# Pooled keys, query loads and value loads moved in an attention and two-layer expert kernel: a change of order

## The chip, the cores and the metric

The kernel runs on one core of one Trainium2 chip. The time is device microseconds (us) of one execution. Five engines appear by these names: PE (TensorE matmuls; PEld is its weight load), DVE (VectorE), ACT (ScalarE), POOL (GpSimd) and SP (SyncE, which here only issues DMAs; SPq is its queue).

## The reference, cut to what matters

Three stages follow each other. Keys and values are summed in groups of eight rows (576 rows become 72) before the attention; the attention's output, 4608 rows of 512, goes through a gated product and two more products, and then through a top-1 mixture of eight experts.

```python
    k_p = k.reshape(B, H, Sp, pool, D).mean(axis=3)
    v_p = v.reshape(B, H, Sp, pool, D).mean(axis=3)
    scores = scale * np.matmul(q, k_p.transpose(0, 1, 3, 2))
    ...
    a = x @ w1
    b = x @ w2
    h = a * b @ w3
    return (h @ w_out).astype(np.float32)
    ...
        mask = e_idx == e
        h = np.maximum(x[mask] @ w1[e], 0.0)
        out[mask] = gate_w[mask, None] * (h @ w2[e])
```

Sizes: batch 8, 8 heads, 576 rows, head dimension 64; 512 x 1024 weights in the middle stage; experts of 512 x 1024 x 512.

## The kernel before, in words

The 4608 rows are nine chunks of 512, a chunk is four tiles of 128. A batch is 576 rows, so chunks and batches do not line up: a chunk touches two batches, and a tile can lie half in one batch and half in the next.

Each chunk goes through a **first product** (`mm1`: eight steps m = 0 to 7, each 24 matmuls against w1 and w2, into PSUM tiles `w`) and a **second product** (`mm_w`: four tiles i = 0 to 3, each 48 matmuls against the folded weight W = w3 times w_out, into `x2ps`). Each product is split into three matmuls of high and low parts. The attention of the chunk that follows is spread between these steps by hooks, which are lists of functions called behind a step.

The attention of a chunk is the class `Attention`. `S(i)` does the scores of tile i (eight matmuls `sc<-kblk,q`, L270; sixteen if the tile lies in two batches) and its softmax (DVE L282 to L293, ACT L290, POOL L299). `K(i)` makes sure that the pooled keys of the batches of tile i stand in `kblk`; this is `prep_k` (four DVE sums `ks<-kr`, L183, and two DVE scalings `kblk<-ks`, L188), which also asks for the next batch's raw keys `kr` (four DMAs, L173). `V1` sums the values on POOL, `T` transposes the softmax, `V` multiplies it with the values. `load_q(t)` asks for the queries of tile t (one DMA, L254, two buffers); `early_v(b)` asks for the raw values of a batch (ten DMAs: four `vr<-v_in` of 256 KB at L195 and six small ones at L199).

In a loop chunk (loop variable ch = 1 to 7) the hooks of `mm1` hold `S(0)` to `S(3)` of chunk ch + 1 behind m = 0 to 3, `V1` behind m = 4 and `T` behind m = 5 to 7. The hooks of `mm_w` hold `V` behind i = 0 and 2 and `early_v` behind i = 3. Behind each i a row block is copied by ACT (`x<-x2ps`, L565), four gate columns are added by DVE (`lg<-x2ps,bias`, L566), and the block is stored (`x2d<-x`, L567, on SP).

The order on each engine in these loop chunks is that of the code, and each engine and SP take their instructions in that order. Chunk 0 (ch = 0, `first_chunk`) and all before it are put in order by a scheduler instead. There the weights are converted: 64-bit words `stage` and `cv` are loaded (L428, L387), passed between ACT (L394, L396), DVE (L397, L399), ACT (L400) and POOL (L122), and w3 and w_out are multiplied (`w_fold`, PSUM tiles `wps`). Small set-up work stands in the same place: a memset `zero` and four stores of it (L526, L528), `bias` (L522 to L524), `tri` (L509).

Of the kernel before, what the change touches and what calls it, by code (L numbers as in the profile page):

```python
# [17 lines left out]
B, H, S, D = 8, 8, 576, 64  # L18
# [74 lines left out]
def _program(outer, tc, nc, I, out):  # L93
# [10 lines left out]
    def mm_ps(name, shape=(P, 512)):  # L104
        return psum.tile(list(shape), F32, name=name, tag="mm", bufs=4)
# [4 lines left out]
    def st4(name, shape, dtype):  # L110
        return st.tile(list(shape), dtype, name=name, tag="st4", bufs=7)

    def st2(name, shape=(P, 512), dtype=F32):
        return st.tile(list(shape), dtype, name=name, tag="st2", bufs=2)
# [77 lines left out]
    def load_v(b, j, vr):  # L192

        if j < 4:
            nc.sync.dma_start(flat(vr), I["v"][b, PK * j:PK * j + P, :])  # L195
        else:
            tail = I["v"][b].rearrange("(a k) x -> a k x", k=PK)[2 * j - 8:2 * j - 6, P:]
            for d in range(3):
                nc.sync.dma_start(flat(vr[2 * TK * d:2 * TK * (d + 1)]), tail)  # L199
# [10 lines left out]
    v_raw = {}  # L210

    def early_v(b):

        if b < B:
            pairs = [st4("vr2", (P, 2, D, POOL), F32) for _ in range(3)]
            v_raw[b] = [pairs[j // 2][:, j % 2] for j in range(6)]
            for j in range(6):
                load_v(b, j, v_raw[b][j])
# [32 lines left out]
    def load_q(t):  # L251
        if t < NT and t not in qs:
            qs[t] = st2("q23", (P, 4, P)) if t in (2, 3) else at.tile([P, 4, P], F32, name="q", tag="q", bufs=2)
            nc.sync.dma_start(qs[t], I["q"][t])  # L254

    def softmax_tile(t):
# [9 lines left out]
        if (r0 + P - 1) // S != r0 // S:  # L266
            segs = [(0, 64, r0 // S), (64, P, r0 // S + 1)]
# [65 lines left out]
    def need(f, b):  # L333
        if b < B and (f, b) not in done:
            done.add((f, b))
            f(b)

    class Attention:
# [19 lines left out]
        def S(self, i):  # L358
            self.K(i)
            self.ex.append(softmax_tile(4 * self.ch + i))  # L360
            load_q(4 * self.ch + i + 1)
            if i < 3:
                self.K(i + 1)

        def T(self, js, banks=None):
# [37 lines left out]
    def run(hooks, n):  # L403
        for f in hooks.get(n, ()):
            f()
# [8 lines left out]
    def prep_w12(m):  # L414
        if m < 8 and m not in done_w:
            done_w.add(m)
            conv(I["w1"][m], flat(wt12[m]["w1h"]), flat(wt12[m]["w1l"]), staged.get((m, "w1")))
            conv(I["w2"][m], flat(wt12[m]["w2h"]), flat(wt12[m]["w2l"]), staged.get((m, "w2")))
# [4 lines left out]
    def stage(srcs):  # L423

        for n, tag in enumerate(("Wh", "Wl")):
            t = wp.tile([P, 4, 512], I64, name="stage", tag=tag)
            for i, (k, src) in enumerate(srcs[4 * n:4 * n + 4]):
                nc.sync.dma_start(t[:, i], src)  # L428
                staged[k] = t[:, i]
# [56 lines left out]
    att = Attention(0)  # L486
# [44 lines left out]
    def mm1(ch, x, hooks):  # L531
        xh, xl = x
        abh = abp.tile([P, 8, 512], F32R, name="abh", tag="abh")
        abl = abp.tile([P, 8, 512], F32R, name="abl", tag="abl")
        for m in range(8):
            w = wt12[m]
            ps = []
            for n in ("w1", "w2"):
                p = mm_ps(n)
                for kb in range(4):  # L540
                    mm3(p, w[n + "h"][:, kb], w[n + "l"][:, kb], xh[:, kb], xl[:, kb], kb == 0, kb == 3)
                ps.append(p)
            a = st2("asb")
            nc.scalar.copy(a, ps[0])
            nc.vector.tensor_tensor(a, a, ps[1], op=ALU.mult)  # L545
            nc.scalar.copy(abh[:, m], a)  # L546
            nc.vector.tensor_tensor(abl[:, m], a, abh[:, m].bitcast(F32), op=ALU.subtract)
            run(hooks, m)
        return abh, abl

    def mm_w(ch, ab, lg, hooks, W):
        abh, abl = ab
        Wh, Wl = W[:2]
        for i in range(4):
            t = 4 * ch + i
            cols = slice(P * i, P * i + P)
            pss = [mm_ps("x2ps") for _ in range(2)]
            for m in range(8):
                for l, r in ((abh, Wh), (abh, Wl), (abl, Wh)):
                    for hf in range(2):  # L560
                        nc.tensor.matmul(pss[hf][:, :260], lhsT=l[:, m, cols], rhs=r[:, m, hf], start=m == 0 and r is Wh and l is abh,  # L561
                                         stop=m == 7 and l is abl)
            x2 = st2("x2")
            for hf in range(2):
                nc.scalar.copy(x2[:, 256 * hf:256 * hf + 256], pss[hf][:, :256])  # L565
                nc.vector.tensor_tensor(lg[:, i, 4 * hf:4 * hf + 4], pss[hf][:, 256:260], bias[:, t, 4 * hf:4 * hf + 4], op=ALU.add)  # L566
            nc.sync.dma_start(x2d[P * t:P * t + P, :], x2)  # L567
            run(hooks, i)
# [44 lines left out]
    lgs = [cst.tile([P, 4, E], F32, name=f"lg{i}") for i in range(2)]  # L613
    def first_chunk():
        att = Attention(1)
        h1 = {m: [lambda m=m: prep_w12(m + 2)] for m in range(8)}
        for n, m in enumerate(S1):
            h1[m].append(lambda n=n: att.S(n))
        h1[0] += [lambda: att.K(0)]
        h1[3] += [lambda: stage(fold[:8])]  # L620
        ab = mm1(0, x_first, h1)
        W = w_fold()
        w_gate(*W)
        for n in range(len(S1), 4):
            att.S(n)
        att.V1()
        load_k(2)
        for js in ((0, 1), (2, 3), (4,)):
            sct = psum.tile([P, 2, 512], F32, name="sct", tag="sc", bufs=1)
            att.T(js, {j: sct[:, j % 2] for j in (0, 1, 2, 3, 4, 5)})  # L630
        prep_routing()
        mm_w(0, ab, lgs[0], {0: [att.V], 2: [att.V], 3: [lambda: early_v(2)]}, W)
        return att.x, W

    def next_chunk(ch, x, W):
        att = Attention(ch + 1)
        r = routing(ch - 1, lgs[(ch - 1) % 2])
        sc = []
        h1 = {0: [lambda: sc.append(place(*r)), lambda: att.S(0)], 1: [lambda: att.S(1), lambda: sc[0](0)],
              2: [lambda: att.S(2)], 3: [lambda: att.S(3), lambda: sc[0](1)], 4: [att.V1],  # L640
              5: [lambda: att.T((0, 1)), lambda: sc[0](2)], 6: [lambda: att.T((2, 3))], 7: [lambda: att.T((4,)), lambda: sc[0](3)]}
        ab = mm1(ch, x, h1)
        b = (512 * (ch + 3) - 1) // S
        mm_w(ch, ab, lgs[ch % 2], {0: [att.V], 2: [att.V], 3: [lambda: early_v(b)]}, W)
        return att.x

    x_first = att.x
    x_cur, W = first_chunk()
# [109 lines left out]
    ch = NC_ - 1  # L758
    ab = mm1(ch, x_cur, {})
# [168 lines left out]
```

## Time and profile before

| | us |
|---|---|
| median of three runs | 1324.92 (1324.34 to 1325.64) |
| the profiled execution | 1322.37 |
| its span, first to last instruction | 1320.6 |
| PE busy | 1236.5 (94% of the span) |
| DVE busy | 676.7 (51%) |
| ACT busy | 381.9 (29%) |
| POOL busy | 405.2 (31%) |

A busy PE is not PE at its peak: a matmul's end is modelled, and matmuls overlap. The granted clock of PE is given as a share of its full speed. Loop chunks 1 to 7 run from 205.7 us to 795.3 us of the span.

### The profile page before, as it was taken

The numbers are of one execution on the slowest core, as the hardware profiler recorded it, in microseconds if no ns is written. First come the engines' busy times: TensorE is split into PE (matmuls) and PEld (weight loads), VectorE is DVE, ScalarE is ACT, GpSimd is POOL, SyncE is SP. The second block draws the span as 40 slices with busy tenths as digits, with TensorE's granted clock in tenths as the row PEclk, the third lists the DMA queues.
The fourth block names the chain that finished last, engine by engine and source line by source line (L and its number), as shares of the span: only waits on it lengthen the run. The fifth ranks groups of instructions, "written<-read, shape, count | busy, mean of one in ns | idle before, by whom it ended". The sixth has DMA issues, their size and how long they took to land. (4 is left out here: it accounts for less than half of the span.)

```text
span 1320.6 us, 17555 instructions
## 1 busy us (share of the span) xinstructions
PE 1236.5 (94%) x6518; PEld 1048.9 (79%) x6518; DVE 676.7 (51%) x1325; ACT 381.9 (29%) x813; POOL 405.2 (31%) x463
## 2 busy tenths in 40 slices
PE   4988798999989989999899999999999999999987
PEld 3766577897978979879789798887888888888877
DVE  6999525436344363343543523745464474556442
ACT  5786532322322223223222221211222212222211
POOL 3576301402314014050140301314543344244242
PEclk7989898999999999999999999998999999999998
DMA  8545212012021130210202001305441442344140
GB/s 291 211 167 202 91 49 80 9 65 79 17 77 52 47 97 9 93 44 25 84 1 87 14 25 50 127 24 184 176 170 46 176 176 95 121 175 168 53 170 18
DMA packets 53371, 126.99 MB, mean 96 GB/s; under 512 B 12668, under 2 KB 12924, under 8 KB 53244
## 3 DMA queue, kind: packets, MB, share of 16 engines
q1 hardware_dynamic: 45884, 105.89, 23.2%
q0 software_dynamic: 7232, 19.71, 3.8%
q8 instruction: 57, 0.93, 0.3%
q14 instruction: 54, 0.44, 0.1%
q10 hardware_dynamic: 144, 0.02, 0.0%
HBM read 105.62 MB, written 20.55 MB: 96 GB/s over the span
## 5 line engine op out<-in xcount | busy, mean ns | idle before, releaser
L299 POOL TENSOR_TENSOR ex<-ex,sm 128x576 f32<-128x576 f32 x35 | 40.5, 1157 | 442.8 <-DVE sm L293 423.7
L117 PE MATMUL e<-xh,e1h 128*128 128x512 f32 (+2 forms) x320 | 122.4, 383 | 5.7 <-issue 4.5
L118 PE MATMUL e<-xl,e1h 128*128 128x512 f32 (+2 forms) x320 | 123.0, 384 | 0.0
L117 PE MATMUL w<-xh,w1h 128*128 128x512 f32 x288 | 120.2, 417 | 1.9 <-ACT w1h L400 1.9
L119 PE MATMUL e<-xh,e1l 128*128 128x512 f32 (+2 forms) x320 | 121.4, 379 | 0.6 <-issue 0.6
L119 PE MATMUL e<-e2h,abl 128*128 128x512 f32 x296 | 117.8, 398 | 3.5 <-DVE abl L738 3.5
L117 PE MATMUL e<-e2h,abh 128*128 128x512 f32 x296 | 118.3, 400 | 1.3 <-DVE abl L738 1.3
L119 PE MATMUL w<-xh,w1l 128*128 128x512 f32 x288 | 115.7, 402 | 2.8 <-POOL w1l L122 2.8
L561 PE MATMUL x2ps<-Wh,abh 128*128 128x260 f32 x576 | 117.4, 285 | 0.3 <-ACT Wh L483 0.3
L561 PE MATMUL x2ps<-Wl,abh 128*128 128x260 f32 x576 | 116.6, 283 | 0.0
L118 PE MATMUL e<-e2l,abh 128*128 128x512 f32 x296 | 116.4, 393 | 0.0
L561 PE MATMUL x2ps<-Wh,abl 128*128 128x260 f32 x576 | 115.9, 283 | 0.0
L117 PE MATMUL w<-xh,w2h 128*128 128x512 f32 x288 | 113.3, 393 | 2.8 <-DVE asb L545 2.8
L118 PE MATMUL w<-xl,w1h 128*128 128x512 f32 x288 | 115.4, 401 | 0.0
L545 DVE TENSOR_TENSOR asb<-asb,w 128x512 f32<-128x512 f32 x72 | 49.4, 686 | 126.2 <-PE w L119 79.4
L119 PE MATMUL w<-xh,w2l 128*128 128x512 f32 x288 | 113.3, 393 | 0.0
L118 PE MATMUL w<-xl,w2h 128*128 128x512 f32 x288 | 112.8, 392 | 0.0
L546 ACT CAST abh<-asb 128x512 fp32r<-128x512 f32 x72 | 44.6, 620 | 192.3 <-DVE asb L545 192.3
L737 ACT ACTIVATE abh<-e 128x512 fp32r<-128x512 f32 (+2 forms) x80 | 45.4, 567 | 169.8 <-PE e L119 157.2
L750 POOL DMA_INDIRECT out<-o,idc x37 | 37.5, 1012 | 182.7 <-ACT o L749 161.9
L566 DVE TENSOR_TENSOR lg<-x2ps,bias 128x4 f32<-128x4 f32 x72 | 11.6, 162 | 155.9 <-ACT x L565 151.9
L561 PEld LDWEIGHTS x2ps<-Wh,abh 128*128 128x128 f32 x576 | 89.3, 188 | 0.7 <-ACT Wh L483 0.4
(203 smaller groups left out, 2650.6 us busy)
## 6 DMA issues: line engine op xcount, KB each, us to landing
raw<-ew_in SPq DMA_DIRECT2D x80, 512.0 KB
stage<-w_in SPq DMA_DIRECT2D x19, 512.0 KB
kr<-k_in SPq DMA_DIRECT2D x32, 288.0 KB
q<-q_in SPq DMA_DIRECT2D x36, 256.0 KB
vr<-v_in SPq DMA_DIRECT2D x36, 256.0 KB
x2d<-x SPq DMA_DIRECT2D x36, 256.0 KB
cv<-w_in SPq DMA_DIRECT2D x13, 512.0 KB
vr<-v_in SPq DMA_DIRECT2D x54, 64.0 KB
```

The source lines that it names most:

```text
L117: nc.tensor.matmul(ps, lhsT=wh, rhs=xh, start=start, stop=False)
L118: nc.tensor.matmul(ps, lhsT=wh, rhs=xl, start=False, stop=False)
L119: nc.tensor.matmul(ps, lhsT=wl, rhs=xh, start=False, stop=stop)
L299: eng.tensor_tensor(e3, e3, bc(sm.unsqueeze(2), [P, H, SP_]), op=ALU.mult)
L545: nc.vector.tensor_tensor(a, a, ps[1], op=ALU.mult)
L546: nc.scalar.copy(abh[:, m], a)
L561: nc.tensor.matmul(pss[hf][:, :260], lhsT=l[:, m, cols], rhs=r[:, m, hf], start=m == 0 and r is Wh and l is abh, stop=m == 7 and l is abl)
L566: nc.vector.tensor_tensor(lg[:, i, 4 * hf:4 * hf + 4], pss[hf][:, 256:260], bias[:, t, 4 * hf:4 * hf + 4], op=ALU.add)
L737: nc.scalar.activation(hT[0][:, m, :w], ps[:, :w], AF.Relu)
L750: nc.gpsimd.indirect_dma_start(out=out, out_offset=bass.IndirectOffsetOnAxis(idc[:, i, 0:1], 0), in_=o, in_offset=None, bounds_check=N - 1 ...
```

## The change

Three edits. The sums of the keys of a batch (and with them the request for the next batch's raw keys) go from `S` into the hook behind i = 1 of the second product of the chunk before; in `S` they stay for chunks 0 and 1 alone. `S(i)` asks for the queries of two tiles ahead, not one. `early_v` does nothing for a batch whose values have been asked for (batch 7 came up twice, at ch = 5 and 6).

```diff
     def early_v(b):
-        if b < B:
+        if b < B and b not in v_raw:
...
             self.ex.append(softmax_tile(4 * self.ch + i))
             load_q(4 * self.ch + i + 1)
-            if i < 3:
+            load_q(4 * self.ch + i + 2)
+            if i < 3 and self.ch < 2:
                 self.K(i + 1)
...
         prep_routing()
-        mm_w(0, ab, lgs[0], {0: [att.V], 2: [att.V], 3: [lambda: early_v(2)]}, W)
+        mm_w(0, ab, lgs[0], {0: [att.V], 1: [lambda: need(prep_k, 2)], 2: [att.V], 3: [lambda: early_v(2)]}, W)
...
         b = (512 * (ch + 3) - 1) // S
-        mm_w(ch, ab, lgs[ch % 2], {0: [att.V], 2: [att.V], 3: [lambda: early_v(b)]}, W)
+        mm_w(ch, ab, lgs[ch % 2], {0: [att.V], 1: [lambda: need(prep_k, b)], 2: [att.V], 3: [lambda: early_v(b)]}, W)
```

The order of PE's matmuls is the same in both programs. Lines behind L362 stand one line further down in the changed kernel (L567 is L568 there). On DVE and SP the order moves.

First place, a loop chunk on SP. Before, from the stores of the second product of ch = 3 to the stores of the next one:

```order
L567 DMA x2d<-x_3767 128x512
L567 DMA x2d<-x_3861 128x512
L567 DMA x2d<-x_3917 128x512
L567 DMA x2d<-x_4001 128x512
L195 DMA vr_4007<-v_in 128x512 x2
L195 DMA vr_4008<-v_in 128x512 x2
L199 DMA vr_4009<-v_in 32x1x512 x6
L254 DMA q<-q_in 128x512 x2
L173 DMA kr<-k_in 128x576 x4
L254 DMA q<-q_in 128x512 x2
```

The same stretch of the changed kernel:

```order
L568 DMA x2d<-x_3769 128x512
L568 DMA x2d<-x_3863 128x512
L173 DMA kr<-k_in 128x576 x4
L568 DMA x2d<-x_3934 128x512
L568 DMA x2d<-x_4018 128x512
L195 DMA vr_4024<-v_in 128x512 x2
L195 DMA vr_4025<-v_in 128x512 x2
L199 DMA vr_4026<-v_in 32x1x512 x6
L254 DMA q<-q_in 128x512 x4
```

The key loads moved from among the query loads to between the second and third store; the four query loads are still behind the values, but each is now for a tile one further on.

Second place, the second product of ch = 2 on DVE. Before:

```order
L566 TENSOR_TENSOR lg_400<-x2ps,bias 128x4 x2
L329 TENSOR_TENSOR xl<-avps,xh 128x256 x4
L240 SCALAR_TENSOR_TENSOR vbl<-vs,c,vbh 128x4x64 x2
L247 SCALAR_TENSOR_TENSOR vbt<-vs,c,vbt 32x2x64 x2
L566 TENSOR_TENSOR lg_400<-x2ps,bias 128x4 x4
```

The changed kernel, same place:

```order
L240 SCALAR_TENSOR_TENSOR vbl<-vs,c,vbh 128x4x64 x2
L247 SCALAR_TENSOR_TENSOR vbt<-vs,c,vbt 32x2x64 x2
L567 TENSOR_TENSOR lg_401<-x2ps,bias 128x4 x2
L183 TENSOR_REDUCE ks<-kr 128x72 x4
L188 TENSOR_SCALAR kblk_87<-ks 64x4x72 x2
L567 TENSOR_TENSOR lg_401<-x2ps,bias 128x4 x2
```

The six key instructions stand between the `lg` pair of the second tile and that of the third.

Third place, SP at the end of `w_fold`, in the part that the scheduler puts in order. In brackets are the semaphores that an instruction waits for: DVE, Pool and PE mean an instruction of that engine, DMAHW an earlier DMA. Before:

```order
L528 DMA x2d<-zero 128x512 [waits DMAHW4_49,DVE_49]
L528 DMA x2d<-zero 128x512 [waits DMAHW5_49]
L528 DMA x2d<-zero 128x512 [waits DMAHW6_49]
L528 DMA x2d<-zero 128x512 [waits DMAHW7_49]
L387 DMA cv<-w_in 128x512 [waits DMAHW0_49,PE_49]
L387 DMA cv<-w_in 128x512 [waits DMAHW1_49,PE_49]
L387 DMA cv<-wo_in 128x512 [waits DMAHW2_49,PE_49,Pool_49]
L387 DMA cv<-w_in 128x512 [waits DMAHW3_49,PE_49,Pool_49]
```

The changed kernel:

```order
L529 DMA x2d<-zero 128x512 [waits DMAHW0_49]
L173 DMA kr<-k_in 128x576 [waits DMAHW1_49,DVE_49]
L173 DMA kr<-k_in 128x576 [waits DMAHW2_49,DVE_49]
L388 DMA cv<-w_in 128x512 [waits DMAHW3_49,PE_49]
L388 DMA cv<-w_in 128x512 [waits DMAHW4_49,PE_49]
L388 DMA cv<-wo_in 128x512 [waits DMAHW5_49,PE_49,Pool_49]
L173 DMA kr<-k_in 128x576 [waits DMAHW6_49,DVE_49]
L388 DMA cv<-w_in 128x512 [waits DMAHW7_49,PE_49,Pool_49]
```

The scheduler has drawn `prep_k(2)` forward from the second product of chunk 0 into `w_fold`. Three of the loads for batch 3 now stand ahead of weight loads, and each waits for a DVE sum of batch 2. On DVE the same six key instructions stand there, one sum earlier in `w_fold` and, in the rows below, the rest behind the memset `zero`:

```order
L527 MEMSET zero 128x512
L398 SCALAR_TENSOR_TENSOR stage<-stage 128x512
L183 TENSOR_REDUCE ks<-kr 128x72
L400 SCALAR_TENSOR_TENSOR stage<-stage 128x512
L183 TENSOR_REDUCE ks<-kr 128x72
L398 SCALAR_TENSOR_TENSOR cv<-cv 128x512
L183 TENSOR_REDUCE ks<-kr 128x72
L400 SCALAR_TENSOR_TENSOR cv<-cv 128x512
L188 TENSOR_SCALAR kblk_87<-ks 64x4x72 x2
```

Before, no sum of batch 2 stood in `w_fold`, and the last of the three `bias` instructions (L524, L525 in the changed kernel) came behind the memset; now it comes ahead of it, and the first of them (L522) stands much further up, behind the casts of `mf`.

## Rows read from the trace of the kernel before

**Rows 1.** The page's first part: busy time, share of the span, instructions.

```profile
PE 1236.5 (94%) x6518; PEld 1048.9 (79%) x6518; DVE 676.7 (51%) x1325; ACT 381.9 (29%) x813; POOL 405.2 (31%) x463
```

**Rows 2.** Waits of PE: who waited for whom, total us, times, longest.

```profile
PE sc L270 <- DMA q<-q_in: 18.7, 6, 4.4
PE sc L270 <- DVE kblk L188: 8.9, 5, 5.1
PE sc L270 <- issue: 8.4, 3, 4.3
```

**Rows 3.** Windows, first products of ch = 1 to 7: us, busy (count), PEclk, DMA.

```profile
205.70:262.90 57.20, 52.92 (x252) 44.22 (x250) 29.48 (x67) 14.27 (x26) 18.63 (x33) 0.94 0.14 42
...
456.90:514.90 58.00, 53.50 (x261) 44.34 (x259) 29.68 (x67) 14.38 (x26) 19.96 (x34) 0.97 0.23 68
...
714.90:768.40 53.50, 50.59 (x252) 42.21 (x251) 26.30 (x62) 14.26 (x26) 11.47 (x16) 1.00 0.15 48
sum 397.30, PE 368.82 PEld 306.16 DVE 204.15 ACT 100.19 POOL 128.28; mean PE 52.69 PEld 43.74 DVE 29.16 ACT 14.31 POOL 18.33
```

**Rows 4.** Timeline of PE in ch = 7: start, us, instruction, [idle <-releaser].

```profile
720.42 1.23 PE L270 MATMUL sc<-kblk,q 128*128 128x144 f32 x8
...
730.04 1.22 PE L270 MATMUL sc<-kblk,q 128*128 128x144 f32 x8 [2.91 <-DMA q<-q_in]
...
736.59 1.14 PE L270 MATMUL sc<-kblk,q 128*128 128x144 f32 x8
```

**Rows 5.** Timeline of all engines in ch = 1, around the second score.

```profile
218.80 2.68 DVE L183 TENSOR_REDUCE ks<-kr 128x72 f32<-128x576 f32 x4
...
221.51 0.62 DVE L188 TENSOR_SCALAR kblk<-ks 64x288 f32<-64x288 f32 x2
...
222.24 2.26 PE L270 MATMUL sc<-kblk,q 128*128 128x144 f32 x8 [4.28 <-issue]
```

**Rows 6.** Timeline of PE in ch = 4, the scores.

```profile
462.44 1.23 PE L270 MATMUL sc<-kblk,q 128*128 128x144 f32 x8
...
473.52 2.26 PE L270 MATMUL sc<-kblk,q 128*128 128x144 f32 x8 [4.37 <-DMA q<-q_in]
...
481.49 2.52 PE L270 MATMUL sc<-kblk,q 128*64 128x144 f32 x16
```

**Rows 7.** Timeline of SP in ch = 4, value and query loads.

```profile
461.62 3.95 SPq L199 DMA_DIRECT2D vr<-v_in  x6
465.62 0.89 SPq L254 DMA_DIRECT2D q<-q_in  x2
```

**Rows 8.** Timeline of DVE in the second product of ch = 2.

```profile
366.31 0.44 DVE L566 TENSOR_TENSOR lg<-x2ps,bias 128x4 f32<-128x4 f32 x2 [5.37 <-ACT x L565]
```

**Rows 9.** View of line L183: durations (ns), DVE's idle time before it.

```profile
L183 DVE TENSOR_REDUCE ks<-kr x32: 700/742/753, 3.8 to 659.6; 128x72 f32<-128x576 f32 x32
...
  DMA kr<-k_in: 3.5, 2
```

**Rows 10.** Timeline of DVE at the end of w_fold.

```profile
128.17 0.44 DVE L522 TENSOR_TENSOR bias<-mf,mb 128x288 f32<-128x288 f32 x1
...
129.04 0.48 DVE L526 MEMSET zero<- 128x512 f32 x1
129.45 0.62 DVE L397 SCALAR_TENSOR_TENSOR stage<-stage 128x512 int32<-128x512 int32 x1
130.00 1.56 DVE L524 TENSOR_TENSOR bias<-bias,btmp 128x288 f32<-128x288 f32 x1
```

**Rows 11.** Timeline of SP, the same place.

```profile
129.56 1.80 SPq L528 DMA_DIRECT2D x2d<-zero  x4
131.45 0.90 SPq L387 DMA_DIRECT2D cv<-w_in  x2
```

**Rows 12.** Timelines of ACT and PE, the same place.

```profile
135.81 0.67 ACT L394 ACTIVATE cv<-cv 128x512 f32<-128x512 f32 x1 [1.62 <-DMA cv<-w_in]
...
139.29 0.50 PE L117 MATMUL wps<-wo,w 128*128 128x512 f32 x1 [2.02 <-ACT w L400]
```

## The prediction

> **What bounds the kernel now.** The page's first part comes first: PE is busy 94% of the span, every other engine at most about half of it [rows 1]. So time can only come from PE's idle stretches, or from matmuls that run at the lower clock. The view of PE's waits names the idle stretches [rows 2]: the scores `sc` (L270) waited 18.7 us for queries, six times, and 8.4 us for "issue", three times, where the view found no releaser. The third row, 8.9 us for `kblk`, lies mostly in the start-up; about 1.4 us of it is in the loop. That makes 28.5 us of idle PE in loop chunks 1 to 7.
>
> What stands behind "issue" is read from a timeline [rows 5]: in chunk 1 DVE does four key sums and two scalings (2.68 + 0.62 us), the last ends at 222.13, and PE, idle for 4.28 us, starts the second score at 222.24. So the key sums stand between two scores of the same chunk and PE waits for them. The queries are read in chunk 4 [rows 6, 7]: SP asks for them at 465.62, behind ten value loads, and PE's second score starts at 473.52, 7.9 us after. A step of the first product takes 6.55 us, score to score (736.59 less 730.04, [rows 4]). A load that is asked for behind one score and takes 7.9 us is too late for the next.
>
> Idle time is not all of the loss. After such a wait the same eight score matmuls took 2.26 us, against 1.22 to 1.23 undisturbed [rows 4 to 6], and the mean granted clock was 0.94 and 0.97 in the stretches of chunks 1 and 4, 1.00 in chunk 7 [rows 3]; full is 2.4 GHz, and what it falls to is 1.2. So I price the loss by the length of the seven first products, not by the gaps.
>
> **The change, part by part.**
>
> *The loop's waits.* The seven first products take 397.3 us together [rows 3]. What one takes without a wait comes from chunk 7, 53.5 us, which kept its clock and has one wait: from its first to its second score 9.62 us pass, from the second to the third 6.55, so the wait costs 3.07 and an undisturbed first product is 50.4 us [rows 3, 4]. Chunks 2, 4 and 6 have one tile that lies in two batches, sixteen small matmuls in 2.52 us instead of eight in 1.22 [rows 6]: 1.3 us each of real work. Undisturbed: 7 x 50.4 + 3 x 1.3 = 356.7. The loss is 397.3 - 356.7 = 40.6 us, of which 28.5 is idle PE and 12 is slow clock and restart. In the ratio of the gaps, some 27 of it belongs to the queries and 14 to the keys. If both waits go, all of it goes, since the matmuls themselves stay in the same order.
>
> Do they go? *Keys:* in chunks 2 to 6 every sum now stands in the second product of the chunk before, with two whole tiles of it (2 x 5.8 us, pair to pair of [rows 8]: 5.37 idle and 0.44 work) still to come before any score. *Queries:* the loads stay behind the values on SP, but the first of them is now for the third score, not the second; the second score's tile was asked for behind the fourth score of the chunk before. In chunk 4, the tightest, the load would land at 473.5 as now, and the third score is due at 462.44 + 2 x 6.55 = 475.5: 2 us to spare. The load of two tiles ahead waits on SP for the score that frees its buffer; queued behind it is only the next query load and, much later, the stores. The doubled values (ten DMAs, about 6 us of SP's time in chunk 6) stood ahead of chunk 7's query load; they go, and that gain is within chunk 7's 3.07.
>
> *What covers the moved sums.* In the second product DVE now has 2.68 + 0.62 = 3.30 us more between the second and third `lg` pair. It sat idle for 5.37 us there, waiting for ACT [rows 8], so 2.1 us remain and the third pair is not late. Cover gone, 3.3 us in each of five chunks would be at stake, 16 us, plus the clock. The key loads that follow wait on SP for these sums, with the third store behind them; that store is not due before the third pair.
>
> *The scheduled part, w_fold.* Here the change costs. The six key instructions of batch 2 are drawn forward into a stretch where PE waits for converted weights (2.02 us, [rows 12]), these wait for `cv` data (ACT 1.62 us, [rows 12]), and SP asked for that data at 131.45, straight behind the four zero stores, which waited for DVE's memset [rows 10, 11]. Now three things come ahead. One sum (0.74, the median of [rows 9]) and the last `bias` (1.56) stand ahead of the memset, the first `bias` (0.44) no longer does [rows 10]: 1.9 us later, the memset ends at 131.4. Behind it DVE does twice a conversion (0.62) and a sum (0.74), 2.7 us, to the end of the third sum at 134.1, and only then can SP issue the second key load and, 0.45 later (half of the 0.90 of two loads, [rows 11]), the first `cv` load: 134.6 instead of 131.45, 3.1 us late. I take 3.1 us, since ACT, DVE and PE behind it all wait for that data in turn. Below, if PE's own pace hid the memset's 1.9: 1.4. Above: all 3.30 us of key work, the 1.9, and a longer PE gap that brings the lower clock, another 3: 8.
>
> In chunk 1 the keys' wait goes with that, and its 4.28 us are in the 40.6. In the start-up query loads move ahead of some weight loads; PE waits there on DVE and ACT, which convert, and I count 0, bounds -1 and +1.
>
> *Sum.* 1322.37 - 40.6 + 3.1 = 1284.9 for the profiled execution. The median of the three runs shown, 1324.92, lies 2.55 above the profiled one, which puts the median after at 1287.4; I round to **1288 us**, 2.8% less.
>
> **A rule of the skill against the trace.** The row says that a query load of 256 KB landed 7.9 us after it was asked for, in the shadow of the values [rows 7, 6]. The Trainium skill, "DMA: Bandwidth & Descriptors", section "Anatomy of one DMA", gives a fit (for the GpSimd path) of about 2.0 us plus bytes over 436 GB/s: an estimate of 2.6 us. By that the load of 465.62 would be there at 468.2, before the second score is due, and asking earlier would bring nothing; the trace does not agree, it names the query DMA as PE's releaser in all six cases. If the rule held in place of the row, only the keys' share would go, and that is the fourth rival.
>
> **Rivals.**
>
> 1. *The query wait moves to the third score.* For it: the load is still issued at the same place of SP's queue, with 2 us to spare in chunk 4. Against: one query load, not two, now follows the values at once. If half of the queries' 27 us stayed: 1288 + 14 = 1302.
> 2. *w_fold costs its upper bound.* For it: the key loads stand in the weight loads' way on SP and in the DMA engines, and DVE is full there. 1288 + 5 = 1293, with the longer gap's clock up to 1296.
> 3. *DVE parks on keys in the second product* (the other side). DVE takes its instructions in order; if the sums found the raw keys not landed, every `lg` behind them would be late, the PSUM tiles would not come free, and PE would stop. The place is the third tile of five second products. PE is covered for the 2.1 us of DVE and one tile of 5.8. To lose the 37.5 us that the rest brings, PE must stand 7.5 us per chunk, so the keys must come 15.4 us late. At 18 us late: 1288 + 5 x 10.1 = 1338, slower. Against: all 32 sums of the kernel waited 3.5 us for keys, twice [rows 9], and the keys are now asked for one second product ahead of the next.
> 4. *The query load is not what holds the second score,* the change does not do what it says: 1322.37 - 14 + 3.1 + 2.55 = 1314. Against: the releaser in [rows 2].
>
> **How the numbers follow.** The forecast gets 0.78, with a range of its own from 1283 to 1293 (w_fold from its lower to its upper bound; loss from 39 to 42). Rival 2 beyond that 0.08, rival 1 0.06, rival 4 0.03, rival 3 0.03, no change at all 0.02. The range runs from 1283 to 1297: forecast and rival 2, 0.86. A measurement of this kernel tells 0.2%, about 2.6 us, from no change. Faster by more: 0.95; within: 0.02; slower: 0.03.
>
> **What would show it.** In the profile after: no score in chunks 1 to 7 waits over 0.5 us; the seven first products take about 357 us at clock 1.00; the query row is gone from PE's waits; in w_fold the wait for ACT's `w` grows from 2.0 to about 5 us and SP's first `cv` load of the last group stands near 134.6; DVE's wait for ACT before the third `lg` shrinks to about 2 us. Wrong would be: a wait for `q` before the third score; DVE idle on `kr` in a second product; PE idle on `lg`; or a w_fold longer by over 8 us.

## The result, and the profile after

| | before | after |
|---|---|---|
| median of four executions, us | 1324.63 (1323.27 to 1325.64) | 1280.16 (1276.81 to 1281.75) |
| ratio, 95% interval | | 0.9662 (0.964 to 0.9683) |
| the profiled execution, us (span) | 1322.37 (1320.6) | 1281.75 (1280.0) |
| first products of chunks 1 to 7 together, us | 397.3 | 355.2 |
| `w_fold`, us | 58.1 | 61.2 |

The change wins 44.5 us, 3.4%. The forecast was 1288 us, with a range from 1283 to 1297: the direction is right, the time is 2.8 us below the range.

The page's first part of the kernel after, to be held against [rows 1], shows PE busier by share and with 14 us less of busy time; 13.6 of them lie in the seven first products, where the same matmuls run at a higher mean granted clock:

```profile
PE 1222.4 (96%) x6518; PEld 1040.2 (81%) x6518; DVE 676.3 (53%) x1325; ACT 380.6 (30%) x813; POOL 404.3 (32%) x463
```

PE's waits over the whole span, to be held against [rows 2]. The rows for queries and for "issue" before a score are gone; the row for `kblk` lies in the start-up. Asked for the seven chunks alone (207 to 755 us), the view has no row at all. The wait for converted weights in `w_fold` is the second thing to see (before, 5.2 us in three waits, the longest 2.0):

```profile
PE sc L270 <- DVE kblk L188: 8.1, 4, 5.1
...
PE wps L117 <- ACT w L401: 5.8, 3, 4.5
```

Windows over the seven first products, to be held against [rows 3] (us, busy time and count of each engine, granted clock, DMA share, GB/s). Every window is full of PE, and the granted clock is 1.00, the 2.4 GHz level, in all of them:

```profile
207.30:257.60 50.30, 50.30 (x251) 42.27 (x250) 26.13 (x61) 14.15 (x26) 19.16 (x34) 1.00 0.11 29
...
441.50:492.70 51.20, 51.20 (x260) 42.70 (x259) 26.78 (x61) 14.27 (x26) 20.29 (x34) 1.00 0.18 54
...
677.50:727.90 50.40, 50.40 (x252) 42.36 (x252) 26.32 (x62) 14.15 (x26) 11.58 (x16) 1.00 0.06 17
sum 355.20, PE 355.20 PEld 297.53 DVE 185.85 ACT 99.30 POOL 129.40; mean PE 50.74 PEld 42.50 DVE 26.55 ACT 14.19 POOL 18.49
```

Timelines of PE and of SP in chunk 4, to be held against [rows 6, 7]. SP comes to the queries at 450.32, behind the ten value loads as before, but PE goes from score to score in steps of 6.5 us, and no row has an idle time in brackets:

```profile
446.98 1.23 PE L270 MATMUL sc<-kblk,q 128*128 128x144 f32 x8
453.54 1.14 PE L270 MATMUL sc<-kblk,q 128*128 128x144 f32 x8
460.08 1.74 PE L270 MATMUL sc<-kblk,q 128*64 128x144 f32 x16
...
450.32 18.51 SPq L254 DMA_DIRECT2D q<-q_in  x4
```

Timeline of DVE in the second product of chunk 2, to be held against [rows 8]. The sums stand between the second and the third pair of `lg`, and DVE's wait for ACT ahead of the third pair has shrunk from 5.37 to 2.08 us, as forecast:

```profile
350.51 0.44 DVE L567 TENSOR_TENSOR lg<-x2ps,bias 128x4 f32<-128x4 f32 x2 [3.83 <-ACT x L566]
350.86 2.72 DVE L183 TENSOR_REDUCE ks<-kr 128x72 f32<-128x576 f32 x4
353.62 0.62 DVE L188 TENSOR_SCALAR kblk<-ks 64x288 f32<-64x288 f32 x2
356.31 0.44 DVE L567 TENSOR_TENSOR lg<-x2ps,bias 128x4 f32<-128x4 f32 x2 [2.08 <-ACT x L566]
```

Timelines of SP, ACT and PE at the end of `w_fold`, to be held against [rows 11, 12]. Key loads now stand ahead of and among the last `cv` loads. ACT starts on the `cv` data at 138.76, 2.95 us later than before, and PE's wait behind it is 4.51 instead of 2.02 us:

```profile
131.00 1.33 SPq L173 DMA_DIRECT2D kr<-k_in  x2
132.43 0.88 SPq L388 DMA_DIRECT2D cv<-w_in  x2
...
138.76 0.65 ACT L395 ACTIVATE cv<-cv 128x512 f32<-128x512 f32 x1 [3.78 <-DMA cv<-w_in]
...
142.22 0.79 PE L117 MATMUL wps<-wo,w 128*128 128x512 f32 x1 [4.51 <-ACT w L401]
```

Over the profiled executions, then: loop -42.1 us, `w_fold` +3.1, and a third part that the prediction did not have, `w_gate` behind `w_fold`. These are the windows of `w_gate`, first of the kernel before, then of after; it is 1.4 us shorter, at a higher mean clock:

```profile
154.70:174.90 20.20, 16.42 (x64) 7.00 (x64) 7.96 (x14) 6.69 (x14) 0.00 (x0) 0.83 0.07 26
```

```profile
157.70:176.50 18.80, 14.97 (x65) 6.84 (x65) 7.99 (x14) 6.66 (x14) 0.00 (x0) 0.91 0.09 28
```

No other stage differs by more than 0.9 us, and the sum is -40.6, from 1322.37 to 1281.75.

### The profile page after: what moved, and what is told of

Read it like the earlier page. It is cut to its first block, busy times and chain, and to the rows that moved or that the text cites. A ratio compares the mean times of both kernels' runs of the same rounds, so it can differ in the third digit from the quotient of the medians.

```text
span 1280.0 us, 17551 instructions
## 1 busy us (share of the span) xinstructions
PE 1222.4 (96%) x6518; PEld 1040.2 (81%) x6518; DVE 676.3 (53%) x1325; ACT 380.6 (30%) x813; POOL 404.3 (32%) x463
## 5 line engine op out<-in xcount | busy, mean ns | idle before, releaser
L751 POOL DMA_INDIRECT out<-o,idc x37 | 37.5, 1013 | 184.2 <-ACT o L750 169.9
L705 DVE CAST e1h<-raw 128x512 fp32r<-128x512 f32 x80 | 70.5, 896 | 36.0 <-DMA raw<-ew_in 35.2
```

The lines of the kernel that those rows point to most:

```text
L705: nc.vector.tensor_copy(h2, r)
L751: nc.gpsimd.indirect_dma_start(out=out, out_offset=bass.IndirectOffsetOnAxis(idc[:, i, 0:1], 0), in_=o, in_offset=None, bounds_check=N - 1 ...
```

## The experiments

All ratios are to the kernel before, run in the same set on the same chip. Five sets gave medians of the kernel before from 1314.17 to 1317.58 us, with 62 executions between 1305.61 and 1326.6, so times of different sets are compared by ratio.

**The three parts alone.** Each leaves one part of the diff in the kernel before. Keys alone:

```diff
-            if i < 3:
+            if i < 3 and self.ch < 2:
...
+ 1: [lambda: need(prep_k, 2)]   (second product of chunk 0)
+ 1: [lambda: need(prep_k, b)]   (second product of chunks 1 to 7)
```

(The last two lines show only the entry that is added to the hooks of `mm_w`.)

> The keys' part of the change alone: sums and next loads in the preceding second product; queries loaded one tile ahead, the last batch's values loaded twice, as in the kernel before. Theory (the two kinds of wait in the loop are separate and their prices add): of the 42.1 us that the loop lost, the keys' waits with the half clock behind them are 4.28 + 3.4 in chunk 1, 1.60 in chunk 3, 2.49 + 1.7 in chunk 5, 1.32 in chunk 6, 14.8 together; less 3.1 us in w_fold. About 1312 us (1310 to 1315); the query waits before second scores stay. Rival (a late query alone holds the scores, keys' sums only wait beside it): nothing comes back in chunks 3 to 6, w_fold costs 3.1, 1320 us or more.

Queries alone:

```diff
             load_q(4 * self.ch + i + 1)
+            load_q(4 * self.ch + i + 2)
```

> The query part alone: queries loaded two tiles ahead; keys' sums in the first product and values twice, as in the kernel before. Theory (additive): the query waits with their half clock, about 27.2 us, go; keys' waits stay, w_fold is as before: about 1297.5 us (1295 to 1300). Rival 1 (the sums take over: with the second score on time VectorE's sums for the third are late by what the query wait had hidden): the waits before third and fourth scores grow by 2 to 3 us in each of chunks 3, 5 and 6, 1303 us or more. Rival 2 (query latency is not what holds the second scores): 1315 us or more.

Values alone:

```diff
-        if b < B:
+        if b < B and b not in v_raw:
```

> The guard against the second load of the last batch's values alone. Theory: only chunk 7 is touched, where the query of the second score lies behind ten value loads that are not needed; its wait of 2.91 us goes, with nothing else: about 1321.7 us. Rival (these loads cost nothing or more elsewhere): 1324.6 us, or over 3 us won.

Measured: keys alone 1302.84 us, ratio 0.9894 (0.9853 to 0.9935), 12.5 us won where 12.6 were expected, but by other parts: the seven first products took 386.4 us, 10.9 less where 14.8 were expected, and `w_fold` 59.2, 1.1 more where 3.1 were expected. Queries alone 1300.38, ratio 0.9889 (0.9863 to 0.9915), 15.0 us won where 27 were expected; first products 380.6. Values alone 1306.42, ratio 0.9939 (0.9914 to 0.9964), 8.9 us won where 2.9 were expected. The sums of the seven first products, of keys, queries and values alone:

```profile
sum 386.40, PE 366.15 PEld 305.18 DVE 184.50 ACT 99.96 POOL 130.69; mean PE 52.31 PEld 43.60 DVE 26.36 ACT 14.28 POOL 18.67
```

```profile
sum 380.60, PE 363.42 PEld 303.19 DVE 205.96 ACT 99.71 POOL 129.60; mean PE 51.92 PEld 43.31 DVE 29.42 ACT 14.24 POOL 18.51
```

```profile
sum 390.90, PE 367.48 PEld 305.38 DVE 204.40 ACT 100.09 POOL 129.88; mean PE 52.50 PEld 43.62 DVE 29.20 ACT 14.30 POOL 18.55
```

PE's waits from chunk 1 to 7, of queries alone:

```profile
PE sc L270 <- issue: 10.3, 3, 4.3
PE sc L270 <- DVE kblk L188: 6.8, 3, 3.1
```

and of keys alone:

```profile
PE sc L270 <- DMA q<-q_in: 20.2, 6, 4.9
```

The waits are not separate. With the queries on time, the scores wait for the keys 17.1 us, where the gaps that the keys held were 4.3 + 1.6 + 2.5 + 1.3 = 9.7 us in the kernel before ([rows 5] has the first): the sums now are the later of two things that had been late together; their waits grew by 3.1, 1.9 and 2.3 us in chunks 2, 3 and 4. Queries alone went the way of rival 1, though that had named chunks 3, 5 and 6. The three parts win 10.9, 16.7 and 3.1 us in the first products (the last is chunk 7 alone, 53.5 to 50.4, as expected), 30.7 in sum, against 42.1 together: 11 us come back only when both late things are mended.

What values alone won beyond chunk 7 is not shown to be its doing. Its other first products were 3.3 us shorter in sum (4.1 shorter in chunks 4 to 6, 0.8 longer in 1 to 3), where the edit moves nothing, and the rest lies for the most part in stages behind the loop which differ between executions of one kernel too (below).

**`w_fold`.** Three versions of the changed kernel. Batch 2's sums put back into chunk 1:

```diff
-            if i < 3 and self.ch < 2:
+            if i < 3 and self.ch < 3:
...
- 1: [lambda: need(prep_k, 2)]   (second product of chunk 0)
```

> The changed kernel, with the sums of the third batch (index 2) alone put back where the kernel before had them, in the first product of chunk 1. Theory (w_fold's longer time is the price of these sums and the loads that they call for): w_fold falls from about 61.5 to 57.5 to 58.1 us, the first product of chunk 1 rises from 50.36 to 57.3, the other six stay at 50.36 and 51.25: 3 to 3.5 us more than the changed kernel, ratio to the kernel before about 0.973. Rival (w_fold's length has another cause): w_fold stays at 61 to 62, and the whole is 7 us more, ratio 0.976 or more.

Only the key loads of batch 3 held back, VectorE's order as in the changed kernel:

```diff
-        if 1 < b < B - 1:
+        if 2 < b < B - 1:
             load_k(b + 1)
...
-  4: [att.V1],
+  4: [lambda: load_k(3), att.V1],
```

> The changed kernel, with the four key loads of the next batch (index 3) taken out of the sums of batch 2, and issued in the first product of chunk 1; SyncE's queue in w_fold is then as in the kernel before, VectorE's as in the changed kernel. Theory 1 (the loads ahead of the last conversion loads in SyncE's queue are what lengthens w_fold): w_fold 57.5 to 58.5 us, the rest unchanged, 3 to 4 us less than the changed kernel. Theory 2 (VectorE's sums between the conversions lengthen it): w_fold stays at 61 to 62 us, no difference to the changed kernel beyond 1 us.

The whole second product of chunk 0 in written order:

```diff
-        mm_w(0, ab, lgs[0], {0: [att.V], 1: [lambda: need(prep_k, 2)], 2: [att.V], 3: [lambda: early_v(2)]}, W)
...
     with tc.manual_schedule(engines={ET.PE, ET.DVE, ET.Activation, ET.Pool, ET.SP}):
+        mm_w(0, ab, lgs[0], {0: [att1.V], 1: [lambda: need(prep_k, 2)], 2: [att1.V], 3: [lambda: early_v(2)]}, W); x_cur = att1.x
         for ch in range(1, NC_ - 1):
```

> The changed kernel, with the second product of chunk 0 inside the part whose order is as written, so that neither the sums of batch 2 nor the key loads of batch 3 are drawn into w_fold. Both theories of w_fold's length: w_fold 57.5 to 58.5 us. Theory (sums and loads find room in this second product as they do in the other seven): that stage stays at 30.8 us give or take 0.5, the first product of chunk 1 at 50.4, and the whole is 3 to 4 us less than the changed kernel. Rival (the order as written is worse there, transposes no longer spread by the scheduler, values loaded late): the stage grows by 2 us or more, or the value sums are late in the next first product, and the gain is gone.

Measured: 1279.21 us, ratio 0.9701 (0.9675 to 0.9728); 1270.37, ratio 0.9641 (0.9616 to 0.9667); 1271.87, ratio 0.9649 (0.9626 to 0.9671). Windows of `w_fold` in these three, in this order:

```profile
95.90:153.40 57.50, 48.77 (x193) 36.30 (x194) 45.72 (x54) 39.08 (x68) 33.55 (x23) 0.97 0.46 171
```

```profile
95.70:153.40 57.70, 48.92 (x192) 36.11 (x193) 48.53 (x60) 39.14 (x68) 33.96 (x24) 0.97 0.46 172
```

```profile
96.10:153.30 57.20, 48.64 (x193) 36.30 (x193) 45.48 (x54) 39.05 (x68) 33.72 (x24) 0.97 0.47 173
```

In the second, VectorE still does the sums in `w_fold` (60 instructions, 48.53 us busy, against 54 and 45.72 without them), and the stage is as short as in the kernel before. So the price of `w_fold` is that of SyncE's four key loads, not of VectorE's sums. Timelines of SP and ACT in this second version say how: `cv` loads asked for at 130.18 are used at 134.33, 4.15 us later; in the changed kernel, with key loads around them, it was 132.43 and 138.76, 6.33 us.

```profile
130.18 0.90 SPq L388 DMA_DIRECT2D cv<-w_in  x2
...
134.33 0.67 ACT L395 ACTIVATE cv<-cv 128x512 f32<-128x512 f32 x1 [0.15 <-DMA cv<-w_in]
```

The run with keys alone parts the two costs. There the first `cv` loads are asked for as late, but with one key load behind them and none directly ahead, and their data is used 4.40 us later; `w_fold` is 1.1 us longer. So about 2 us of the price are data that come slower with two key loads directly ahead, and 1 us is the later request:

```profile
132.50 0.90 SPq L387 DMA_DIRECT2D cv<-w_in  x2
133.50 0.40 SPq L387 DMA_DIRECT2D cv<-wo_in  x1
133.99 0.38 SPq L173 DMA_DIRECT2D kr<-k_in  x1
...
136.90 0.66 ACT L394 ACTIVATE cv<-cv 128x512 f32<-128x512 f32 x1 [1.82 <-DMA cv<-w_in]
```

With batch 2 late, chunk 1's first product was 56.5 us (57.3 expected), and the other six undisturbed, as expected; the whole was put at a ratio of about 0.973 and came to 0.9701, no more than the changed kernel's own 0.9701 and 0.9706 in other sets (below). In written order the second product of chunk 0 kept its 30.7 us: the rival there falls.

The kernel before was run once more for a trace, on the same chip.

> The kernel before, unaltered, for its trace on this chip. On the chip of the first four runs its executions had a median of 1315.35 us, where the four shown had 1324.63. Theory (chips and executions differ outside the loop): the seven first products add up to 397 us give or take 2 as in [rows 5], and the difference lies in the stages after the loop, whose waits for transfers are shorter. Rival (the half clock behind the loop's waits comes and goes): the stages after the loop are as in the profiled execution, and the seven first products add up to 392 us or less.

Its profiled execution took 1319.75 us, where its set had a median of 1317.58. Windows of its seven first products, their sum (the row meant in the expectation is the sum in [rows 3]):

```profile
sum 397.10, PE 369.30 PEld 307.02 DVE 206.60 ACT 100.16 POOL 128.96; mean PE 52.76 PEld 43.86 DVE 29.51 ACT 14.31 POOL 18.42
```

The loop is the same to 0.2 us in the two traces; the 2.6 us between them lie elsewhere: chunk 8's first product is 3.4 us shorter (46.1 instead of 49.5), all else together 0.8 us longer.

**The changed kernel again.** Two sets with it unaltered, and one with the held key loads beside it.

> The changed kernel itself, unaltered. Disputed: that its profiled execution (1281.75 us) lay above the other three, where that of the kernel before lay below all its others. Theory (chance of one execution): executions spread over 1277 to 1282 us with the profiled one anywhere among them, the mean granted clock higher where the time is shorter; median 1279 to 1281. Rival (the profile itself costs or gives a fixed amount): the profiled execution stands at the same end again, 1.5 us or more above the median of the others.

> The changed kernel once more, unaltered, beside the next run on the same chip, and for a third sample of the difference to the kernel before, which was 44.5 us in the four executions shown and 38.4 us on the chip of the first four runs. Theory (loop 42.1 us, w_fold 3 to 4 us against it; all else is what executions differ by in the stages before and after the loop): seven first products 355.2 us, difference 36 to 41 us, ratio 0.969 to 0.973. Rival (the change wins several us outside the loop as well): difference 43 us or more, ratio 0.9675 or less.

> The changed kernel with the key loads of batch 3 held back to the first product of chunk 1, unaltered from its first run, beside the changed kernel on the same chip. Theory (these four loads cost 3 to 4 us in w_fold): 3.5 to 6.5 us less than the changed kernel here, w_fold 57 to 58.5 us against 61 to 62. Rival (its 1270.37 us was a good draw of executions): within 2 us of the changed kernel.

Measured: 1276.96 us (1273.63 to 1280.04), ratio 0.9706 (0.9681 to 0.9731), 38.4 us won; 1278.19 (1277.16 to 1280.67), ratio 0.9701 (0.9672 to 0.9731), 39.0 us won; held key loads 1274.28, ratio 0.9671 (0.9641 to 0.9702), 3.9 us less than the changed kernel beside it. The seven first products took 355.2 us in all three traces. What executions of one kernel differ by is shown by two windows, chunk 8's first product and the first quarter of the expert matmuls. The changed kernel, profiled with 1281.75 us:

```profile
754.80:804.00 49.20, 46.50 (x203) 37.90 (x202) 23.82 (x62) 9.72 (x19) 13.52 (x12) 0.97 0.20 70
828.20:946.50 118.30, 113.32 (x499) 91.47 (x498) 65.91 (x160) 23.80 (x41) 47.73 (x42) 0.97 0.38 137
```

and again, with a span of 1274.3 instead of 1280.0 us:

```profile
754.70:801.50 46.80, 45.06 (x205) 36.81 (x203) 24.12 (x62) 9.80 (x19) 13.11 (x12) 1.00 0.21 74
825.60:940.60 115.00, 112.91 (x499) 91.11 (x499) 67.02 (x160) 23.80 (x41) 48.14 (x42) 0.99 0.39 140
```

These two stages make 5.7 us, as much as the whole difference of the spans. The kernel before has the same two kinds of stage, 46.1 or 49.5 us in chunk 8's first product in its two traces. That the change wins several us outside the loop, the rival in the third sample, falls by both ratios.

**Why the query load is late.** Three versions of the kernel before. The ten value loads in another order:

```diff
-            for j in range(6):
+            for j in (4, 5, 0, 1, 2, 3):
                 load_v(b, j, v_raw[b][j])
```

> The kernel before, with the order of a batch's ten value loads turned round: the six loads of 64 KB first, the four of 256 KB behind them; the query load that holds the second score is issued behind all ten, as before. Disputed: why that query takes 7 to 8 us. Theory (the six small loads go over few DMA engines, and the query's packets on these engines stand behind them): with four full-width loads between them and the query, the query lands within about 4 us, the waits before second scores (2.6, 3.4, 4.4, 2.4, 2.9 and 2.9 us in chunks 2 to 7) go to under 1 us; as in the run with queries two tiles ahead, the sums of the keys take part of it over, so about 15 us less than the kernel before, ratio 0.988 to 0.990. Rival (bytes: 1.4 MB stand ahead of the query, whatever their order): the waits stay within 0.5 us of these, ratio 0.998 to 1.002.

The queries on another queue:

```diff
-            nc.sync.dma_start(qs[t], I["q"][t])
+            (nc.scalar if t > 8 else nc.sync).dma_start(qs[t], I["q"][t])
...
-            self.K(i)
+            self.K(i); self.ch > 1 and load_q(4 * self.ch + i + 1)
```

> The kernel before, with the queries from tile 9 on loaded through ScalarE's DMA queue instead of SyncE's, each issued ahead of the exponential of the tile before; ScalarE comes to that place at about the time at which SyncE had issued it (about 297.7 in chunk 2), so only the queue differs, not the time of issue. Disputed: why the query that follows ten value loads needs 7 to 8 us. Theory (it stands behind them in its own queue): on another queue it lands within 3 to 4 us, the waits before second scores fall under 1 us, the keys' waits take over as in the run with queries two tiles ahead, about 15 us less than the kernel before, ratio 0.987 to 0.990. Rival (the DMA engines themselves are full with the values' 1.4 MB, whichever queue asks): waits of 2 to 4.5 us stay in chunks 2 to 7, ratio 0.998 or more.

The small loads with another first dimension (`ext` and the masks in `constants()` are permuted with it):

```diff
-            tail = I["v"][b].rearrange("(a k) x -> a k x", k=PK)[2 * j - 8:2 * j - 6, P:]
+            tail = I["v"][b].rearrange("(a k) x -> a k x", k=PK)[2 * j - 8:2 * j - 6, P:].rearrange("a k x -> k a x")
```

> The kernel before, with the six small value loads of a batch read with the sixteen keys as the first dimension of the source, where it was two heads; masks and the attention's tail columns are permuted to match; the order of all queues and the number of all instructions are as before. Disputed: why a query behind the ten value loads takes 7 to 8 us when their order does not matter and another queue frees it. Theory (these loads go over few of the DMA engines, and the query's packets wait on these): the waits for queries fall from 18.7 us to under 4 in all, the keys' waits take over as on the other queue, ratio 0.987 to 0.993. Rival (the bytes ahead in the queue, however spread): waits of 2 to 4.5 us stay in chunks 2 to 7, ratio 0.998 to 1.002. The Trainium skill, DMA: Bandwidth & Descriptors, section Why a DMA increments its semaphore by 16 and not by 1, is on the theory's side: it has the number of engines as the largest common divisor, up to 16, of both sides' slowest dimensions, 2 for these loads as they were and 16 with the edit.

PE's waits for queries in chunks 1 to 7, another order first, then another queue:

```profile
PE sc L270 <- DMA q<-q_in: 21.3, 6, 4.1
```

```profile
PE sc L270 <- DMA q<-q_in: 1.2, 2, 0.6
```

With another first dimension the view has no such row, only the keys':

```profile
PE sc L270 <- issue: 10.3, 3, 4.3
PE sc L270 <- DVE kblk L188: 6.8, 3, 3.1
```

Measured: order 1320.47 us, ratio 1.0022 (0.9998 to 1.0046); queue 1304.55, ratio 0.9927 (0.9903 to 0.9951); first dimension 1295.5, ratio 0.9857 (0.9828 to 0.9886). What the order was expected to change did not come: with the small loads first, the second score started 7.2 to 8.0 us after its query was asked for, as in the kernel before (7.5 to 8.2), and all ten stand ahead of it in the queue either way. On ScalarE's queue the wait is nearly gone (1.2 of 18.7 us), so they hold it up in their own queue, not by filling the DMA engines for all queues; 9.6 us were won there, where about 15 were expected. And with the same bytes, the same order and the same queue, spread by their first dimension, the small loads hold nothing up: not the bytes, but how the six loads of 64 KB are laid out. In chunk 2 SP asked for the query at 291.64, and the second score started at 296.88 without a wait. The view of the DMAs lists 2.9 us from issue to landing for this load, and a median of 3.0 for the 26 query loads of the window from 203 to 760 us:

```profile
291.64 0.58 SPq L254 DMA_DIRECT2D q<-q_in  x1
...
296.88 1.20 PE L270 MATMUL sc<-kblk,q 128*64 128x144 f32 x8
```

```profile
q<-q_in SPq DMA_DIRECT2D x1, 256.0 KB, 2.9
```

What the small loads do shows in the same view. It has the mean busy share of the 16 DMA engines in tenths, here in 40 slices of 0.225 us around the query of chunk 2. The kernel before, 297 to 306 us (the query asked for at 297.77), with PE's second score and a window of the low stretch (the last two numbers are the DMA share and the GB/s):

```profile
DMA  1111111122799311111111111111111111100875
```

```profile
305.50 3.76 PE L270 MATMUL sc<-kblk,q 128*64 128x144 f32 x16 [2.62 <-DMA q<-q_in]
```

```profile
300.50:304.70 4.20, 2.38 (x11) 1.64 (x9) 3.35 (x7) 1.16 (x2) 0.72 (x1) 1.00 0.13 51
```

The query on ScalarE's queue, the same 297 to 306 us (asked for at 297.20, the score not waiting at 302.87):

```profile
DMA  1111169885111111111111111111111111000558
```

Another first dimension, 291 to 300 us (asked for at 291.64):

```profile
DMA  5714508373597200000000000000000000000876
```

Before, the small loads keep a share of 0.13 of the engines busy, at 51 GB/s; at that rate their 393 KB take 7.7 us, an estimate. A short burst comes between 299.0 and 300.2, but the low level goes on to 304.9, and the score starts 0.6 us later. On the other queue the burst comes too, and the score does not wait for the low level to end; with the other first dimension there is no such level, and all has come by 294.2. So most of the query comes in the burst, and a part of it stands behind the small loads on the few engines that these use. The view gives the mean of all engines and not each one, so this last step is the reading that fits the three traces, not a row.

The Trainium skill, "DMA: Bandwidth & Descriptors", section "Why a DMA increments its semaphore by 16 and not by 1", says that a load runs on as many engines, up to 16, as the largest number that divides the slowest dimension of both its sides: 2 for the small loads as they were, 16 with the edit. The trace agrees: two of 16 engines are a share of 0.125, and the window above has 0.13.

The edit also shortened what lies ahead of `w_fold`, where value loads stand among the weight loads, from 96.6 to 91.7 us, and the seven first products from 397.3 to 383.3, which makes up nearly all of its 19.4 us, more than the other queue won. So it was tried on the best version, the changed kernel with the key loads held back.

> The changed kernel with the key loads of batch 3 held back, and with the small value loads spread as in the run beside it. Theory (in the loop no score waits any more, so nothing is to be had there; only the value loads of batches 0 and 1, which stand among the weight loads ahead of w_fold, could gain): within 1 us of the version with the loads held back alone, ratio 0.963 to 0.968. Rival (the small loads held up weights in the start-up as well): w_fold or the stretch before it 2 us or more shorter, ratio 0.962 or less.

Measured: 1266.04 us (1264.65 to 1270.98), ratio 0.9629 (0.9607 to 0.9651), the fastest of all. Of the rival the stretch ahead of `w_fold` came true: it is 92.3 us (95.7 with the loads held alone). But in these two traces nearly all of it is given back, in `w_fold` (59.2 instead of 57.7) and in `w_gate` (19.4 instead of 17.8), which ends at 170.9 us instead of 171.2. The windows of `w_gate`, first with the loads held alone, then with the small loads spread as well:

```profile
153.40:171.20 17.80, 13.89 (x64) 6.11 (x64) 8.03 (x14) 6.74 (x14) 0.00 (x0) 1.00 0.10 29
```

```profile
151.50:170.90 19.40, 15.50 (x65) 6.21 (x65) 8.00 (x14) 6.66 (x14) 0.00 (x0) 0.91 0.09 27
```

Against the held loads' 0.9641 and 0.9671 the ratio does not settle whether the step pays there.

## Why the prediction was right in direction and wrong in size

*The loop's waits: right.* No score waits in chunks 1 to 7, none moved to the third score (rival 1), the query load was what held the second (rival 4 falls), DVE did not park on keys (rival 3), and DVE's spare 2.1 us ahead of the third `lg` pair came out at 2.08. The loop's share of the `kblk` row was 1.3 us, not 1.4, which changes nothing in the sum. An undisturbed first product was priced at 50.4 us and took 50.4. One size in the term was off: a tile that lies in two batches was priced at 1.3 us, from a 2.52 us row of [rows 6]; it takes 1.74 us where its neighbours take 1.14 to 1.23, and the chunks that hold one are 0.9 us longer than the others. The 2.52 us stood behind a query wait, one tile later, and were set against 1.22 us of an undisturbed tile; in the second trace of the kernel before the same tile took 1.74 us. Three such chunks and rounding make 355.2 instead of 356.7: 1.5 us. That the loss goes as one, not in two shares, the runs of single parts showed; the 27 and 14 us by ratio of the gaps were no prices (16.7 and 10.9 alone).

The fit in the Trainium skill, "DMA: Bandwidth & Descriptors", section "Anatomy of one DMA", an estimate of 2.6 us for that load, is near the 2.9 us that it took once the small loads were spread, though the page has the fit for the GpSimd path and this load is SyncE's; that section says nothing of what stands ahead in the queue, and that was the case here.

*`w_fold`: the sum right, the way there wrong.* The 3.1 us were met in the profiled execution; in two other traces it was 3.6 to 3.8. But the step had the first `cv` load at 134.6, behind a memset that was to end 1.9 us late, and three sums. The memset ended at 129.06, 0.5 us earlier than before; the load was asked for at 132.43, 1.0 us late, and its data came 2 us slower, with key loads ahead of it in the queue. Holding back those loads alone gave all of it back. The data in the key loads' way are the mechanism of rival 2, at the forecast's price: that the two errors cancelled is luck.

*`w_gate`: put at nothing.* The 1.4 us that the profiled pair showed were not in the sum. The stage took 20.2 and 20.3 us in the two traces of the kernel before and 18.8, 19.1 and 19.1 in the three of the changed kernel; but four versions of the kernel before with edits elsewhere took 19.2 to 20.4, and all traces 17.8 to 20.4, at granted clocks of 1.00 to 0.83. That the change itself shortens this stage is not shown.

*The step that failed: "which puts the median after at 1287.4".* Three terms lie in it: the offset of the profiled execution, the loop's 1.3 us for a split tile, and `w_gate`, which had no term. The first is the largest. The prediction carried the kernel before's own offset, profiled execution 2.55 us under the median, over to the kernel after, as if it belonged to the profile. It is a draw. The profiled execution after lay 1.6 us above the median, one more of the kernel before 2.2 above its set's, and two more of the kernel after 0.9 below and 2.5 above theirs. So the miss of 7.2 us from 1287.4 to 1280.16 is 2.55 + 1.6 of offsets, 1.5 of the loop, 1.4 of `w_gate`, and 0.2 of all else. The predicted difference of the profiled executions, 37.5 us, was measured as 40.6, and as 38.4 and 39.0 between medians of later sets. By the ratios of those sets the same 1324.63 us would have become 1285 to 1286, an estimate, inside the range: that the time lay below it was in part the draw of these executions.

*The range.* It was made of the costs of the change alone. Executions of one kernel within a set spread over 2 to 16 us, and the four of the kernel before that the result is held against lay at 1323 to 1326, where five later sets had medians of 1314 to 1318. Why those four lay so high is open: the one trace from beside them has the loop of the later one.

## What to carry to other kernels

Take what two late things cost from what the stage takes without either, since the waits of a pair hide one another: mended alone they were worth 10.9 and 16.7 us, and with a third, small one 42.1 together. Before a load is moved ahead, look at what stands in front of it in its queue; in the kernel before, spreading six small loads by their first dimension took away the query waits that asking earlier did, and shortened the stretch ahead of `w_fold` by 4.9 us too. When work is moved into code that a scheduler orders, look where its transfers land: four key loads drawn into `w_fold` took back 3 to 4 us, and a forecast in microseconds wants the spread of executions in its range.

## What was not expected of the hardware

Six loads of 64 KB made a 256 KB load behind them late in one queue (7 to 8 us from request to score, waits of 2.4 to 4.4 us), whether they were the last or the first of ten, hardly from another queue (waits of 0.6 us) and not at all with sixteen as the first dimension (2.9 us to landing). While the small loads ran, the DMA engines' mean share was 0.13. The granted clock of the same stage differs between executions of one kernel: 0.97 in one trace of the changed kernel and 1.00 in another in chunk 8's first product, with 2.4 us between them, while the seven windows without a wait were at 1.00 in every trace of the changed kernel.
